# A fused attention and two-MoE kernel: a third value buffer, key and query loads three units ahead, and the pooled values' product moved one unit forward

## Chip, cores and metric

The kernel runs on one core of a Trainium2 chip. The metric is device time in microseconds (us) of one execution. Lower is better. TensorE is called PE, VectorE DVE, ScalarE ACT, GpSimd POOL; SP is the engine whose queue issues nearly all loads.

## What is computed

Three layers follow each other on 2304 tokens of width 512. The change touches the first alone: for 4 batches and 8 heads, an attention over mean-pooled tokens (groups of 4, 144 of them) is repeated to full length and added to a local attention in a band of 3 to each side. A soft MoE and a top-2 MoE (8 experts of 512x1024x512 each) come after it.

```python
q_d, k_d, v_d = (t.reshape(B, H, Sd, 4, D).mean(axis=3) for t in (q, k, v))
out_up = np.repeat(sm_attn(q_d, k_d, v_d), 4, axis=2)
scores = np.where(abs(pos[:, None] - pos[None, :]) < 4, scale * q @ k.T, -1e9)
x = out_up + softmax(scores) @ v
x = soft_moe(x, phi, w1, w2)          # 8 experts, 4 slots each
out = top2_moe(x, w_gate, w_noise, noise, w1, w2)
```

## The kernel before

**Units.** The attention is cut into 16 units, one for each batch and pair of heads. The work of a unit u is cut into named steps, and a table BL gives each step its function and an offset: at pass p of the loop over units (lines 592 to 615) a step with offset o works on unit p - o. The string SEQ (lines 19 and 20) is the order in which a pass writes its steps; every engine runs its own instructions in just that order, for a manual schedule is in force. The last pass is written out by TSEQ (lines 21 to 24), with a unit's number beside each step.

**The steps that matter here.** `ld` (load, line 186) issues four loads of a unit's keys and queries from SP, each of 96x6x64 floats in rows of 256 bytes (147,456 bytes); the tile `ld` has two buffers. `A0` and `A1` (a_pe) transpose keys and queries on PE (line 236) into PSUM tiles `t`, of which there are four; `a00`, `a01` and `a100` to `a111` copy them to K and Q. `S` (b_s) makes the local scores (lines 287, 292), `SD` (b_d) the pooled ones (line 303). `CP`, `CD` transpose the two probabilities; `EP00` to `EP11`, `ED0`, `ED1` copy them to PT and PdT. `lV` (load_v, line 202) issues four loads of a unit's values, each of 64x5x64 floats in rows of 256 bytes (81,920 bytes). `VD` (v_pe) pools the values, `V0`, `V1` copy the pooled values to Vd. `DP` (d_pe, line 416) is the local product of probabilities and values, `DD` (d_d, line 423) the pooled one; both go to the PSUM tiles xa and xb. `x0`, `x1` copy the local result to xT, `XA` (d_add, line 435) adds the pooled one to it. `EP`, `X0`, `X1`, `LG`, `LA` turn the result and multiply it with the router of the first MoE; once in four units `SE`, `ST`, `SS`, `SU_`, `SK` bring a batch into that MoE's slots.

**Who copies.** Function cp (line 222) sends a PSUM copy to ACT, unless its name is in the list ON_V (line 26): then DVE does it.

**Loads beside the attention.** `W` issues loads of the first MoE's weights (8 matrices of 2 MB in halves of 1,048,576 bytes, numbers 0 to 7) at a rate that NW (line 29) gives for each pass: one half a pass. Eight small loads (gate weights and noise, rows of 32 bytes) go out one a pass from pass 5 on. Values alternate between two buffers, so `lV` of unit u waits for `DP` of unit u - 2. Step R2 of TSEQ closes the attention's pools and loads weights 8 to 10 (w8a to w10b) into their place; weights 11 to 15 follow in the buffers of weights 0 to 4 as the first MoE's matmuls (lines 800 and 824) set them free. The second MoE's weights follow on the same queue.

The table's lines that place the moved steps:

```python
BL = {"ld": (load, -2, ()), "lV": (load_v, -1, ()), ...
      "DP": (d_pe, 1, ()), "DD": (d_d, 2, ()), "XA": (d_add, 2, ()), ...
for p in range(-1, NU - 1):
    if p >= 5 and small:
        o, i = small.pop(0)
        nc.sync.dma_start(out=o, in_=i)
    for nm in SEQ:
        f, off, a = BL.get(nm, (None, 99, ()))
        ...
            f(p - off, *a)
        if nm == "W" and p >= 0:
            flush(NW[p])
```

Of the kernel before, what the change touches and what calls it, by code (L numbers as in the profile page):

```python
# [7 lines left out]
F32 = mybir.dt.float32  # L8
# [10 lines left out]
SEQ = """DM ld S DD A0 M a00 a01 A1 a110 XA a100 SD EL a101 ST a111 SK CP SS EX W VD EP01 MD V0 EP00 EP10 SU_ LG CD EP11  # L19
EP V1 LA ED0 DX SU KD ED1 DP lV x1 x0 DQ1 X0 SE DQ0 RD P0 X1 P1""".split()  # L20
TSEQ = """S:15 DD:13 XA:13 DM:14 CP:14 W EP01:14 EP00:14 SD:15 M:15 EL:15 EP10:14 EX:15 EP11:14 CD:14 ED0:14 MD:15 SU:15 VD:14 DP:14 V0:14 V1:14 EP:13
# [4 lines left out]
ON_V = ['k1', 'd1', 'a101', 'a111', 'v0']  # L26
ON_V_END = ['P0', 'k1', 'v0', 'v1']

NW = [1] * 15
# [9 lines left out]
def attn_moe_moe_kernel(ctx: ExitStack, tc: tile.TileContext, q, k, v, moe_phi, moe_w1, moe_w2,  # L39
                        w_gate, w_noise, noise, w1, w2, out, dbg=None):  # L40
    nc = tc.nc
    B, H, S, D = q.shape
    NT = B * S
    DM = H * D
# [73 lines left out]
    with ExitStack() as tctx:  # L118
# [37 lines left out]
        Vs = [(a1, a2)[i].tile([128, 5, 2, D], F32, name=f"V{i}") for i in range(2)]  # L156
# [45 lines left out]
        def load_v(u):  # L202
            b, hp = units[u]
            V = Vs[u % 2]
            hv = v[b, 2 * hp:2 * hp + 2]
            for h in range(2):
                for g2 in range(2):

                    j0, j1 = int(u == h == g2 == 0), 5 - int(u == NU - 1 and h == g2 == 1)
                    rows = slice(64 * g2, 64 * g2 + 64)  # L210
                    t0 = 58 * (2 * j0 + g2) - 3
                    nc.sync.dma_start(out=V[rows, j0:j1, h], in_=bass.AP(
                        tensor=hv.tensor, offset=hv.offset + (h * S + t0) * D,
                        ap=[[D, 64], [116 * D, j1 - j0], [1, D]]))
                    if j0:
                        nc.sync.dma_start(out=V[3:64, 0, h], in_=hv[h, 0:61])
                    if j1 < 5:
                        nc.sync.dma_start(out=V[64:121, 4, h], in_=hv[h, S - 57:S])

# [46 lines left out]
        def v_pe(u):  # L266

            V = Vs[u % 2]
# [138 lines left out]
        def d_pe(u):  # L407
            b, hp = units[u]
            V = Vs[u % 2]
# [139 lines left out]
        def ok(u):  # L549
            return 0 <= u < NU  # L550

        load(0)

        BL = {"ld": (load, -2, ()), "lV": (load_v, -1, ()), "EP": (e_pe, 2, ()), "LG": (logit_pe, 2, ()),
# [8 lines left out]
              "DD": (d_d, 2, ()), "XA": (d_add, 2, ()), "VD": (v_pe, 1, ()), "V0": (v_evac, 1, (0,)), "V1": (v_evac, 1, (1,)),  # L563
# [28 lines left out]
        for p in range(-1, NU - 1):  # L592
            if p == 0:
                nc.sync.dma_start(out=phi, in_=moe_phi.rearrange("(k p) s -> p k s", p=128))
            if p >= 5 and small:
                o, i = small.pop(0)
                nc.sync.dma_start(out=o, in_=i)
# [812 lines left out]
```

## Time and profile before

| | |
|---|---|
| time, median of 3 runs | 489.71 us (487.59 to 493.68) |
| profiled execution: its time | 488.25 us |
| profiled execution: its span | 486.5 us |
| around the span (difference) | 1.75 us |
| PE, DVE, ACT, POOL busy in the span | 94%, 57%, 56%, 46% |
| attention: first local scores of unit 0, of unit 15 | 6.98 us, 137.51 us |
| first matmul of the first MoE | 159.94 us |
| end of the first MoE's second layer | 192.42 us |
| first matmul of the top-2 MoE's output layer (line 1061) | 208.90 us |

The span runs from the first to the last instruction. A busy time is a sum over an engine's instructions. PE's ends are modelled, so a matmul that stands still inside a run of matmuls can count as busy. In a timeline a row is a run of like instructions: its start, its length, engine, line, operation, tiles, sizes, how many; in square brackets the idle time of the engine ahead of it and what ended that.

### The profile page before, as it was taken

Reading aid. Unit: us, or ns where it says so; the run is one execution under the profiler, and the core shown is the slowest. Engines: PE = TensorE matmul, PEld = TensorE weight load, DVE = VectorE, ACT = ScalarE, POOL = GpSimd, SP = SyncE. Lnnn points to the kernel's source line nnn. Section 1 sums busy time; section 2 is a strip of 40 time slices with the busy share of each in tenths; the row PEclk is TensorE's granted clock in tenths of the full one; section 3 lists DMA queues with packets and bytes.
Section 4 is the critical chain, followed back from the end, with each engine's and each line's share of the span. In section 5 each row is a group of like instructions: output and inputs, shape, how many; then the busy total and the mean of one; then the engine's idle time right before and its main releaser. Section 6 shows DMA issues by size and latency. Waiting matters only on the chain.

```text
span 486.5 us, 12430 instructions
## 1 busy us (share of the span) xinstructions
PE 458.1 (94%) x4765; PEld 355.7 (73%) x4765; DVE 275.1 (57%) x703; ACT 270.5 (56%) x699; POOL 221.9 (46%) x321
## 2 busy tenths in 40 slices
PE   6999998899888999999999999999999999999992
PEld 5788877778765543577777887887887877878882
DVE  6888676887875321886487463382552634615300
ACT  2687777777765112674484453672755646727310
POOL 7897667577631201084766677222222222212232
PEclk9999899999999999999999999999999999999998
DMA  8999999899979999999986843799958855333333
GB/s 161 234 245 204 249 207 204 222 224 232 251 212 377 378 394 395 372 341 353 355 236 183 244 67 62 214 357 265 274 98 220 201 129 139 45 43 45 44 44 46
DMA packets 107977, 104.19 MB, mean 214 GB/s; under 512 B 67722, under 2 KB 77642, under 8 KB 107914
## 3 DMA queue, kind: packets, MB, share of 16 engines
q1 hardware_dynamic: 101002, 90.50, 62.5%
q0 software_dynamic: 6912, 12.85, 17.6%
q8 instruction: 40, 0.66, 0.6%
q14 instruction: 23, 0.19, 0.1%
HBM read 83.60 MB, written 19.73 MB: 212 GB/s over the span
## 4 chain that ended last, share of the span: by engine, by line
PE 42%; issue 8%; POOL 2%; POOLq 2%; DVE 1%; DMA 1%; ACT 1%; DVEq 0%
PE y L1061 34%; PE gx L878 2%; PE h L1041 2%; POOL out_dram L1080 2%; POOLq L1086 1%; PE gx L1041 1%; DMA out_dram<-ys,idx 1%; PE xs L944 1%; DVE hl L1043 1%; PE xs L1022 0%; PE xs L941 0%; ACT ys L1072 0%; DVE wlo L1033 0%; PE gx L958 0%; ACT hh L1042 0%
## 5 line engine op out<-in xcount | busy, mean ns | idle before, releaser
L1061 PE MATMUL y<-whi,hl 128*128 128x512 f32 x320 | 127.3, 398 | 0.0
L1061 PE MATMUL y<-whi,hh 128*128 128x512 f32 x320 | 126.6, 396 | 0.4 <-ACT hh L1042 0.4
L1061 PE MATMUL y<-wlo,hh 128*128 128x512 f32 x320 | 126.6, 396 | 0.0
L1080 POOL DMA_INDIRECT out_dram<-ys,idx x40 | 64.6, 1614 | 108.5 <-ACT ys L1072 62.6
L1072 ACT ACTIVATE ys<-y,gt 128x512 f32<-128x512 f32 x40 | 27.4, 686 | 83.7 <-issue 46.9
L1033 DVE TENSOR_TENSOR wlo<-wr,whi 128x512 fp32r<-128x512 f32 x64 | 42.0, 692 | 49.3 <-ACT whi L1030 41.7
L1061 PEld LDWEIGHTS y<-wlo,hh 128*128 128x128 f32 x320 | 60.1, 188 | 12.9 <-issue 1.0
L1061 PEld LDWEIGHTS y<-whi,hl 128*128 128x128 f32 x320 | 60.1, 188 | 12.3 <-issue 2.1
L1061 PEld LDWEIGHTS y<-whi,hh 128*128 128x128 f32 x320 | 60.2, 188 | 11.8 <-ACT hh L1042 0.6
L1007 POOL DMA_INDIRECT tab<-stk,pos x36 | 35.8, 994 | 11.5 <-issue 10.4
L1043 DVE SCALAR_TENSOR_TENSOR hl<-h,hh 128x256 fp32r<-128x256 f32 (+1 forms) x64 | 31.4, 490 | 16.0 <-ACT hh L1042 10.6
L1043 DVE SCALAR_TENSOR_TENSOR hl<-gx,hh 128x256 fp32r<-128x256 f32 (+1 forms) x64 | 31.2, 488 | 10.7 <-ACT hh L1042 7.4
L1030 ACT ACTIVATE whi<-wr 128x512 fp32r<-128x512 f32 x64 | 36.9, 625 | 0.2
L1042 ACT ACTIVATE hh<-gx 128x256 fp32r<-128x256 f32 (+1 forms) x64 | 28.1, 439 | 15.0 <-PE gx L1041 12.0
L1042 ACT ACTIVATE hh<-h 128x256 fp32r<-128x256 f32 (+1 forms) x64 | 28.0, 437 | 12.5 <-PE h L1041 9.5
L236 PE MATMUL t<-idf,ld 96*128 96x96 f32 x192 | 23.7, 270 | 11.8 <-DMA ld<-in_q_dram 5.6
L1079 POOL MEMSET spacer<- 1x1 f32 x40 | 13.5, 338 | 40.9 <-issue 40.9
L236 PEld LDWEIGHTS t<-idf,ld 96*128 96x128 f32 x192 | 18.8, 153 | 16.4 <-DVE fa L166 4.3
L254 POOL TENSOR_TENSOR s<-Q 64x288 f32<-64x288 f32 x31 | 29.3, 945 | 2.4
L336 POOL TENSOR_TENSOR P<-El,su 64x350 f32<-64x350 f32 x31 | 24.4, 787 | 11.4 <-DVE Vd L226 4.9
L224 ACT ACTIVATE PT<-t 64x384 f32<-64x384 f32 (+1 forms) x64 | 25.9, 429 | 6.2 <-PE t L378 5.0
L926 DVE TENSOR_TENSOR oh<-iot,R 128x256 fp32r<-128x256 f32 (+2 forms) x50 | 20.5, 446 | 12.7 <-PE xs L944 10.3
(312 smaller groups left out, 877.9 us busy)
## 6 DMA issues: line engine op xcount, KB each, us to landing
wr<-in_moe_w_dram SPq DMA_DIRECT2D x88, 256.0 KB
wr<-in_moe_w_dram SPq DMA_DIRECT2D x40, 512.0 KB
wr<-in_moe_w_dram SPq DMA_DIRECT2D x16, 1024.0 KB
out_dram<-zero SPq DMA_DIRECT2D x20, 256.0 KB
V<-in_v_dram SPq DMA_DIRECT2D x62, 80.0 KB
ld<-in_k_dram SPq DMA_DIRECT2D x32, 144.0 KB
ld<-in_q_dram SPq DMA_DIRECT2D x32, 144.0 KB
XT<-tab SPq DMA_DIRECT2D x5, 320.0 KB
```

What stands on the lines that cost most here:

```text
L224: nc.scalar.activation(dst, src, AF.Copy)
L236: nc.tensor.transpose(t[:, 96 * c:96 * c + 96], ld[:, i, 3 * j + c].rearrange("p h d -> p (h d)"), idf[0:96, 0:96])
L254: nc.gpsimd.tensor_tensor(q2, q4[:, :, 0:2], q4[:, :, 2:4], op=ALU.add)
L336: eng.tensor_tensor(P[as_, :, HQ * a:HQ * a + KW], El[as_], su[as_, :, None].to_broadcast([64, NG, KW]), op=ALU.mult)
L1007: st = nc.gpsimd.indirect_dma_start(out=tab, out_offset=bass.IndirectOffsetOnAxis(ap=pos[:, c, i:i + 1], axis=0), in_=stk[:, i].bitcast(F3 ...
L1030: nc.scalar.activation(whi[:, kk], wb(kk), AF.Copy)
L1033: eng.tensor_tensor(wlo[:, kk], wb(kk), whi[:, kk].bitcast(F32), op=ALU.subtract)
L1042: nc.scalar.activation(hh[:, f], h, AF.Relu)
L1043: nc.vector.scalar_tensor_tensor(hl[:, f], h, 0.0, hh[:, f].bitcast(F32), op0=ALU.max, op1=ALU.subtract)
L1061: nc.tensor.matmul(y, l[:, kk, ts_], r_[:, kk], start=(m == 0), stop=(m == 23))
L1072: nc.scalar.activation(ys, YS.pop((e, ti)), AF.Copy, scale=gt[:, ti:ti + 1])
L1080: st = nc.gpsimd.indirect_dma_start(out=out, out_offset=bass.IndirectOffsetOnAxis(ap=idx[:, ti:ti + 1], axis=0), in_=ys, in_offset=None, c ...
```

## The change

1. Values have three buffers in place of two, so `lV` of unit u waits for `DP` of unit u - 3.
2. `ld` loads unit p + 3 at pass p (before: p + 2), and stands in SEQ behind `A1`, which frees its buffer; units 0 and 1 are both loaded ahead of the loop. `lV` and `W` come right behind it. SP's queue has them in the order keys and queries, values, weights.
3. NW gives no weight half to pass 0, one to passes 1 to 12 and two to passes 13 and 14. The eight small loads go out four at a time, at passes 13 and 14.
4. `DD` and `XA` have offset 1: they work on the unit whose `DP` stands in the same pass, and leave TSEQ's head for unit 13.
5. SEQ is another order, and ON_V holds other copies: p10, p11 (two copies to PT) and k0 (128x512 to xK) go to DVE, a111 (a copy to Q), v0 (Vd 128x128), d1 (PdT 16x288) and k1 (64x128 to xK) to ACT.

```diff
-SEQ = """DM ld S DD A0 M a00 a01 A1 a110 XA a100 SD EL a101 ST a111 SK CP SS EX W VD EP01 MD V0 EP00 EP10 SU_ LG CD EP11
+SEQ = """S A0 A1 ld lV W M a101 SD DM a00 SS a01 EL a100 a110 ST SK a111 CP EP01 EP10 EP11 VD EP00 MD KD SU_ LG CD V1 V0
...
-ON_V = ['k1', 'd1', 'a101', 'a111', 'v0']
+ON_V = ['p10', 'p11', 'k0', 'a101']
...
-NW = [1] * 15
+NW = [0] + [1] * 12 + [2] * 2
...
-        Vs = [(a1, a2)[i].tile([128, 5, 2, D], F32, name=f"V{i}") for i in range(2)]
+        Vs = [(wk, a1, a2)[i].tile([128, 5, 2, D], F32, name=f"V{i}", bufs=1) for i in range(3)]
...
-            V = Vs[u % 2]
+            V = Vs[u % 3]
...
         load(0)
-
-        BL = {"ld": (load, -2, ()), "lV": (load_v, -1, ()), "EP": (e_pe, 2, ()), "LG": (logit_pe, 2, ()),
+        load(1)
+
+        BL = {"ld": (load, -3, ()), "lV": (load_v, -1, ()), "EP": (e_pe, 2, ()), "LG": (logit_pe, 2, ()),
...
-              "DD": (d_d, 2, ()), "XA": (d_add, 2, ()), "VD": (v_pe, 1, ()), "V0": (v_evac, 1, (0,)), "V1": (v_evac, 1, (1,)),
+              "DD": (d_d, 1, ()), "XA": (d_add, 1, ()), "VD": (v_pe, 1, ()), "V0": (v_evac, 1, (0,)), "V1": (v_evac, 1, (1,)),
...
-            if p >= 5 and small:
+            for _ in range(4 if p >= NU - 3 else 0):
```

**SP, one pass in the middle of the attention.** Before, the queue of SP reads as follows; `ld` are keys and queries, V0 and V1 the two value buffers, `wr` a weight half.

```order
L191 DMA ld_493<-in_k_dram 96x6x64 x2
L191 DMA ld_493<-in_q_dram 96x6x64 x2
L102 DMA wr_169<-in_moe_w1_dram 128x2x1024
L212 DMA V1_136<-in_v_dram 64x5x64 x4
L191 DMA ld_667<-in_k_dram 96x6x64 x2
L191 DMA ld_667<-in_q_dram 96x6x64 x2
L102 DMA wr_170<-in_moe_w1_dram 128x2x1024
L212 DMA V0_135<-in_v_dram 64x5x64 x4
```

And now, with V0, V1 and V2 in turn:

```order
L191 DMA ld_541<-in_k_dram 96x6x64 x2
L191 DMA ld_541<-in_q_dram 96x6x64 x2
L212 DMA V0_135<-in_v_dram 64x5x64 x4
L102 DMA wr_174<-in_moe_w1_dram 128x2x1024
L191 DMA ld_715<-in_k_dram 96x6x64 x2
L191 DMA ld_715<-in_q_dram 96x6x64 x2
L212 DMA V1_136<-in_v_dram 64x5x64 x4
L102 DMA wr_175<-in_moe_w1_dram 128x2x1024
```

The kinds and counts of a pass are the same; the values stand ahead of the weight half, the keys and queries are those of one unit later, and the values' buffer is one that was read a unit earlier.

**PE, from one unit to the next.** The difference on PE where the local product of one unit (line 416) meets the next unit's local scores (lines 287, 292):

```order
 L416 MATMUL xa<-PT,V_135 64x58 x2
 L416 MATMUL xb<-PT,V_135 64x58 x2
+L423 MATMUL xb<-PdT,Vd 64x144 x4
 L287 LDWEIGHTS idb
 L287 MATMUL S<-mask,idb 64x350
@@ -59,5 +60,4 @@
 L287 MATMUL S<-mask,idb 64x350
 L292 MATMUL S<-K,Q 64x35 x20
-L423 MATMUL xb<-PdT,Vd 64x144 x4
 L236 MATMUL t<-idf,ld 128x96 x12
```

The pooled product (four matmuls) moves from behind the next unit's scores to the place right behind the local product; nothing else on PE changes its place within a unit.

**ACT, one unit.** Before, ACT runs a unit without slot work in this order:

```order
L224 ACTIVATE K<-t 128x288 x2
L224 ACTIVATE Q<-t 64x288 x2
L322 ACTIVATE El<-El 128x350
L224 ACTIVATE PT<-t 64x3x128 x2
L224 ACTIVATE PT<-t 64x2x128 x2
L224 ACTIVATE Vd<-xb 16x128
L224 ACTIVATE PdT<-t 128x288
L354 ACTIVATE Ed,sumd<-Sd,nmd 96x144 x3
L224 ACTIVATE xT<-xb 128x5x58
L224 ACTIVATE xT<-xa 128x5x58
L224 ACTIVATE xK<-t 128x4x128
```

And now:

```order
L224 ACTIVATE K<-t 128x288 x2
L224 ACTIVATE Q<-t 64x288 x3
L224 ACTIVATE PT<-t 64x3x128 x2
L224 ACTIVATE Vd<-xb 16x128
L224 ACTIVATE Vd<-xa 128x128
L322 ACTIVATE El<-El 128x350
L224 ACTIVATE PdT<-t 128x288
L224 ACTIVATE PdT<-t 16x288
L354 ACTIVATE Ed,sumd<-Sd,nmd 96x144 x3
L224 ACTIVATE xT<-xa 128x5x58
L224 ACTIVATE xT<-xb 128x5x58
L224 ACTIVATE xK<-t 64x128
```

Both inputs of the pooled product (Vd and PdT) now come from ACT alone, each behind more work than before, and the exponential of the local scores (El) comes behind the copies to PT.

## Rows read from the trace of the kernel before

**Rows 1.** Stretches: length, busy PE, PEld, DVE, ACT, POOL, granted clock, DMA share, GB/s.
```profile
20.00:36.00 16.00, 15.49 (x325) 13.71 (x320) 13.07 (x35) 13.37 (x43) 14.63 (x23) 1.00 1.01 245
20.00:136.00 116.00, 106.44 (x2118) 91.16 (x2113) 91.18 (x231) 87.58 (x284) 83.35 (x121) 0.99 1.01 229
...
136.00:144.00 8.00, 6.64 (x154) 5.75 (x155) 5.49 (x15) 4.53 (x15) 2.45 (x3) 1.00 0.54 142
144.00:192.00 48.00, 46.59 (x745) 23.88 (x735) 16.94 (x61) 14.69 (x41) 7.94 (x32) 1.00 1.03 385
...
48.00:50.00 2.00, 1.22 (x10) 1.09 (x11) 1.04 (x2) 0.71 (x2) 0.60 (x1) 0.88 0.84 286
50.00:52.00 2.00, 2.00 (x12) 1.99 (x11) 0.91 (x2) 1.22 (x3) 0.07 (x1) 0.50 1.12 316
52.00:54.00 2.00, 2.00 (x40) 1.72 (x38) 1.81 (x3) 1.16 (x3) 1.61 (x3) 0.77 1.06 150
```

**Rows 2.** PE's timeline in the attention, some units.
```profile
22.46 0.34 PE L287 MATMUL S<-mask,idb 128*64 128x350 bf16 x2
...
23.77 0.69 PE L423 MATMUL xb<-PdT,Vd 128*64 128x144 f32 x8
...
29.85 0.34 PE L287 MATMUL S<-mask,idb 128*64 128x350 bf16 x2
...
56.41 0.34 PE L287 MATMUL S<-mask,idb 128*64 128x350 bf16 x2
...
65.36 0.34 PE L287 MATMUL S<-mask,idb 128*64 128x350 bf16 x2
...
118.94 0.34 PE L287 MATMUL S<-mask,idb 128*64 128x350 bf16 x2
...
122.51 0.69 PE L236 MATMUL t<-idf,ld 96*128 96x96 f32 x6 [0.93 <-DMA ld<-in_q_dram]
...
127.45 0.34 PE L287 MATMUL S<-mask,idb 128*64 128x350 bf16 x2
...
137.51 0.34 PE L287 MATMUL S<-mask,idb 128*64 128x350 bf16 x2
```

**Rows 3.** PE's waits from 14 to 140 us: total, times, longest.
```profile
PE t L236 <- DMA ld<-in_q_dram: 5.3, 7, 1.1
PE S L292 <- issue: 1.8, 2, 1.4
PE t L236 <- DMA ld<-in_k_dram: 1.0, 2, 0.6
```

**Rows 4.** SP's timeline at the attention's end.
```profile
130.61 0.60 SPq L102 DMA_DIRECT2D wr<-in_moe_w_dram  x1
137.59 2.61 SPq L212 DMA_DIRECT2D V<-in_v_dram  x4
...
141.20 3.41 SPq L104 DMA_DIRECT2D w8a<-in_moe_w_dram  x4
...
161.07 3.91 SPq L104 DMA_DIRECT2D wr<-in_moe_w_dram  x8
```

**Rows 5.** Copies that change engine, 20 to 137 us: busy, mean ns, idle before.
```profile
L224 ACT ACTIVATE Q<-t 64x288 f32<-64x288 f32 x26 | 11.2, 432 | 6.5 <-PE t L236 5.3 <-POOL s L262 0.8
...
L224 ACT ACTIVATE PT<-t 64x256 f32<-64x256 f32 x28 | 10.4, 372 | 0.3
...
L224 ACT ACTIVATE xK<-t 128x512 f32<-128x512 f32 x12 | 7.1, 595 | 0.0
...
L226 DVE COPY PdT<-t 16x288 f32<-16x288 f32 x13 | 5.0, 383 | 0.0
...
L226 DVE COPY Vd<-xa 128x128 f32<-128x128 f32 x14 | 3.9, 279 | 0.0
...
L226 DVE COPY xK<-t 64x128 f32<-64x128 f32 x12 | 3.0, 253 | 0.0
```

**Rows 6.** ACT's timeline: the copy to PdT ahead of the scores at 118.94 us.
```profile
117.72 0.38 ACT L224 ACTIVATE PdT<-t 128x288 f32<-128x288 f32 x1
```

More of the change, by code (lines that the diff above doesn't have):

```diff
@@ L17 @@
 CAP = 640
-SEQ = """DM ld S DD A0 M a00 a01 A1 a110 XA a100 SD EL a101 ST a111 SK CP SS EX W VD EP01 MD V0 EP00 EP10 SU_ LG CD EP11
-EP V1 LA ED0 DX SU KD ED1 DP lV x1 x0 DQ1 X0 SE DQ0 RD P0 X1 P1""".split()
-TSEQ = """S:15 DD:13 XA:13 DM:14 CP:14 W EP01:14 EP00:14 SD:15 M:15 EL:15 EP10:14 EX:15 EP11:14 CD:14 ED0:14 MD:15 SU:15 VD:14 DP:14 V0:14 V1:14 EP:13
+SEQ = """S A0 A1 ld lV W M a101 SD DM a00 SS a01 EL a100 a110 ST SK a111 CP EP01 EP10 EP11 VD EP00 MD KD SU_ LG CD V1 V0
+EP EX DP ED0 ED1 LA X0 DX DD x0 x1 X1 SE DQ0 DQ1 SU RD P0 XA P1""".split()
+TSEQ = """S:15 DM:14 CP:14 W EP01:14 EP00:14 SD:15 M:15 EL:15 EP10:14 EX:15 EP11:14 CD:14 ED0:14 MD:15 SU:15 VD:14 DP:14 V0:14 V1:14 EP:13
 ED1:14 P0:15 P1:15 DD:14 DX:15 LG:13 X0:13 RD:15 x0:14 DM:15 x1:14 CP:15 LA:13 EP00:15 X1:13 EP01:15 EP11:15
@@ L266, in v_pe @@
         def v_pe(u):
-            V = Vs[u % 2]
+            V = Vs[u % 3]
             XL[u] = [ps.tile([128, 512], F32, name=n) for n in ("xa", "xb")]
@@ L408, in d_pe @@
             b, hp = units[u]
-            V = Vs[u % 2]
+            V = Vs[u % 3]
             xl = XL[u]
```

## Prediction, made blind

> **What bounds the kernel now.** I read the stretches first, then PE's timeline in the attention, then PE's waits, then SP's timeline. The stretches [rows 1] show two regimes. From 20 to 136 us, the attention, the load engines are busy all the time (share 1.01) but move only 229 GB/s; from 144 to 192 us, while the first MoE's weights stream, the same share moves 385 GB/s. The attention's rows of 256 bytes are what is slow. PE is busy 106.44 of 116.00 us in the attention, so PE and loads both stand near their limit there, and neither alone explains the time.
>
> PE's timeline [rows 2] tells them apart. One unit runs from one row of line 287 to the next. With nothing late a unit takes 29.85 - 22.46 = 7.39 us. A unit with slot work takes 65.36 - 56.41 = 8.95 us, 1.56 more. A unit in which the queries arrive late takes 127.45 - 118.94 = 8.51 us, 1.12 more, of which 0.93 is shown as idle, waiting on `ld`. From unit 2 (22.46) to unit 15 (137.51) there are 115.05 us for 13 units, three of them with slot work; at the undisturbed pace they would take 13 x 7.39 + 3 x 1.56 = 100.75. So at most 14.3 us can be won between these two marks. PE's waits [rows 3] explain part: 5.3 + 1.0 = 6.3 us for queries and keys, in nine waits; 1.8 us are "issue", which no load named here ends.
>
> [...]
>
> **Why the loads are late.** Before, a unit's `ld` goes out one pass ahead of its use and behind the values of the unit before, and those values wait until the local product two units back has freed their buffer. At the end this shows most plainly: SP issues a weight half at 130.61 and the last values only at 137.59 [rows 4]; the stretch from 136 to 144 us moves 142 GB/s at a share of 0.54 [rows 1].
>
> **The change part by part**, against the profiled execution (488.25 us: 486.5 of span and 1.75 around it).
>
> *Loads one unit earlier, three value buffers.* No bytes are added. Keys now have about two passes to arrive in, some 15 us in place of 7, and values wait for a product that is long over. All nine waits on `ld` should go: -6.3. A late unit loses 1.12 for 0.93 of idle, a fifth more than is shown: another -1.3. The fall of the clock followed such waits (PE's idle stretch at 48 to 50 us): -1.7. Together -9.3; the bounds are 0 (the loads only queue longer) and the whole 14.3 of excess.
>
> *What is late next: the load engines themselves.* A unit's loads are 4 x 147,456 + 4 x 81,920 + 1,048,576 = 1,966,080 bytes. From 20 to 36 us, while PE kept its pace, they moved 245 GB/s at a share of 1.01 [rows 1]; at that rate a unit takes 8.02 us, 0.63 more than PE's 7.39. Over passes 1 to 12 that is a debt of 12 x 0.63 = 7.6 us. Pass 0 loads no weights now, which gives 1.05 MB at 385 GB/s = 2.7 back, and the two slot units among them give 2 x 1.56 = 3.1. What is left, 1.8 us, I charge: +1.8, with bounds 0 and +7.6.
>
> The row for 20 to 36 us leaves 8.02 - 2.72 = 5.3 us for 917,504 bytes in rows of 256 bytes, 173 GB/s [rows 1]. [...]
>
> *Two weight halves in passes 13 and 14, and the small loads there.* Those passes have no keys to load, so the 2.7 us of the second half takes the place of `ld`. Ahead of the values of unit 15 stand eight small loads and two extra halves; these values are first used by `VD` in the last pass, behind that unit's scores, more than a pass later. I take 0. If the cover goes, the price is one half, +2.7.
>
> *The pooled product and the add at their own unit's end.* The product takes 0.69 us and starts 23.77 - 22.46 = 1.31 us behind the scores [rows 2]; now it comes in front of them. PE does as much as before: the last pass loses one product (-0.69), pass 1 gains one (+0.69). What is added is a wait: PE stands at it until ACT has copied both PdT parts and both Vd parts, and the next unit's scores and key transposes are queued behind it on PE, then ACT's and POOL's work on those keys. Before, PdT's larger copy ended at 117.72 + 0.38 = 118.10 and the scores began at 118.94 [rows 2, 6], 0.84 us later. Ahead of the end of the second PdT copy, ACT now has one Q copy, one Vd copy and the small PdT copy more, and two small PT copies less: 0.432 + 0.279 + 0.383 - 2 x 0.372 = +0.35 [rows 5]. So PdT is whole about 0.5 us before PE comes to the product, which stands where the scores stood. I charge +0.3 in all. The bounds are -0.7, if pass 1's product hides in that pass's own waits, and 14 units x 0.38 = +5.3, if PE waits out one whole PdT copy each time.
>
> *Copies that change engine.* ACT loses 2 x 0.372 + 0.595 = 1.34 us a unit and gains 0.432 + 0.279 + 0.383 + 0.253 = 1.35 [rows 5], with DVE's durations taken for ACT; DVE the reverse. ACT is busy 13.37 of 16.00 us at PE's pace [rows 1], so 1.2 us of each 7.39 stay free: 0, covered by that.
>
> *Behind the attention.* Weights 8 to 10 fill the place of the attention's tiles and weights 11 to 15 wait until the first MoE's matmuls free their buffers: the first such load went out at 161.07, in a stream that had not paused since 144 us [rows 1, 4]. If all before it lands sooner than PE arrives, the stream pauses there and has to start again: +0.8, between 0 and +1.1, the time from the first MoE's first matmul (159.94) to that load's issue. Everything later moves with PE's arrival, for the load queue runs on behind it in the same order.
>
> *Sum:* -9.3 + 1.8 + 0.3 + 0.8 = -6.4, so 481.85 us for an execution like the profiled one. That one lies 1.46 us under the median of the runs, so the median comes to 489.71 - 6.4 = 483.3 us. A measurement of this kernel tells about 2% (9.8 us) from no change.
>
> **The rivals.**
>
> *The load engines are already full.* For it: a share of 1.01 over the whole attention [rows 1], and depth adds no rate. A unit then stays at 115.05 / 13 = 8.85 us. Only the hole from 136 to 144 us closes, worth 8 x (1 - 142 / 385) = 5.0 us of loading, but PE's last pass does not wait for those bytes, so little comes of it: I give it -0.7, 489.0 us. Against it: the 245 GB/s of 20 to 36 us at that same share.
>
> *The pace is PE's throughout.* If the debt is covered by the head start and the "issue" idles vanish with the crowding, unit 15's scores come at 22.46 + 100.75 = 123.2 in place of 137.51: -14.3, +0.8 for the restart, 476.2 us; 475 to 480 when a few waits stay. For it: three units in a row at that pace early on. Against it: the debt of 0.63 a unit.
>
> *The pooled product becomes the wait, and the kernel slower.* Place: line 423, now between local product and next scores, behind ACT's longer chain. If ACT, once the loads no longer hold PE back, runs late by as much as a late unit loses today (1.12 us, rows 2), 14 units cost 15.7 us; less the 6.4 won that is +9.3, 499.0 us. It decides from 6.4 / 14 = 0.46 us a unit on, and makes the kernel 2% slower from 1.16. For it: the margin of half a microsecond is worked out, not seen. Against it: ACT's free 1.2 us a unit.
>
> **How the numbers follow.** Forecast (480 to 487.5) 0.47; load engines full 0.20; PE's pace throughout 0.22; pooled product slower 0.11. Faster by over 2% means under 479.9: nearly all of the third case and a little of the first, 0.27. Slower by over 2% means over 499.5: the upper half of the last, 0.06. Within 2%: 0.67. The range goes from 475.5, inside the third case, to 491.0, which takes in the second and leaves out most of the last. The forecast's own range is 480 to 487.5.
>
> **What would show it.** [...] Wrong: waits on `ld` as long as before (engines full), waits of PE at line 423 on ACT's copies of PdT or Vd of half a microsecond and more, or an earlier end of the attention that is lost again between the first MoE and the top-2 MoE.

## The result, and the profile after

The changed kernel takes 495.28 us (491.89 to 498.52, 20 runs), the kernel before beside it 490.77 us (487.19 to 494.87, 20 runs). The ratio is 1.0109, with an interval of 1.0085 to 1.0133: slower by about 1%, which is less than 2% and yet clear of the noise. I had forecast 483.3 us and a range of 475.5 to 491.0; the change went the other way. The ratios, here and below, are those of fast executions and are not the quotient of the two medians.

The profiled execution of after took 496.65 us (span 494.2). It lies 1.4 us above the median of after, and the profiled one of before (488.25) 2.5 us under the median beside it: the two traces are 8.4 us apart where the medians are 4.5 apart. So marks from these two traces show where time is lost, and overstate how much.

The stretches of after, with the columns of [rows 1]:

```profile
2.00:20.00 18.00, 12.77 (x136) 10.39 (x137) 13.52 (x33) 6.07 (x19) 12.04 (x25) 1.00 0.86 165
20.00:36.00 16.00, 16.00 (x310) 14.20 (x308) 13.30 (x33) 12.51 (x42) 14.66 (x22) 1.00 0.89 194
20.00:136.00 116.00, 110.42 (x2191) 97.23 (x2189) 86.89 (x225) 86.63 (x304) 85.34 (x124) 0.97 0.92 210
136.00:144.00 8.00, 6.43 (x146) 5.62 (x138) 5.95 (x18) 4.96 (x20) 3.21 (x4) 1.00 0.93 286
144.00:156.00 12.00, 9.05 (x157) 6.24 (x158) 5.89 (x23) 6.84 (x22) 1.15 (x2) 1.00 0.75 269
156.00:192.00 36.00, 33.41 (x509) 14.60 (x503) 9.25 (x31) 5.92 (x12) 3.59 (x26) 1.00 1.04 394
...
110.00:112.00 2.00, 2.00 (x41) 1.93 (x38) 0.75 (x1) 0.49 (x2) 0.59 (x1) 0.51 0.73 225
```

Two stretches of before that stand in no group:

```profile
2.00:20.00 18.00, 15.09 (x167) 12.35 (x167) 14.15 (x40) 6.41 (x20) 14.26 (x28) 1.00 1.04 209
144.00:156.00 12.00, 10.59 (x198) 7.45 (x192) 7.47 (x29) 8.77 (x29) 2.39 (x3) 1.00 1.02 376
```

PE is busier in the attention than before (110.42 against 106.44 us, though some of it at a lower clock: 0.97), as the forecast wanted. The load engines are not: their share fell from 1.01 to 0.92 and the rate from 229 to 210 GB/s [rows 1]. By 136 us they have moved (209 - 165) x 18 + (229 - 210) x 116 = 3.0 MB less; by 156 us, with the rows for 136 to 156 us, it is 3.1 MB.

PE's waits from 14 to 150 us:

```profile
PE xb L423 <- issue: 2.2, 1, 2.2
PE xa L273 <- DMA V<-in_v_dram: 1.9, 1, 1.9
PE t L378 <- POOL P L336: 1.6, 1, 1.6
PE t L378 <- POOL kd L263: 1.2, 1, 1.2
PE t L236 <- DMA ld<-in_q_dram: 0.9, 1, 0.9
PE S L292 <- issue: 0.8, 1, 0.8
```

Of the 6.3 us on keys and queries [rows 3], 0.9 are left. But the first MoE shows what came of it. PE's timeline there:

```profile
159.92 2.37 PE L801 MATMUL hp<-wr,sinT 128*32 128x256 f32 x40
...
187.64 0.64 PE L801 MATMUL hp<-wr,sinT 128*32 128x256 f32 x8 [0.64 <-DMA wr<-in_moe_w_dram]
...
191.00 1.05 PE L825 MATMUL yacc<-wr,hz 128*32 128x512 f32 x2 [0.29 <-DMA wr<-in_moe_w_dram]
...
193.36 6.14 PE L825 MATMUL yacc<-wr,hz 128*32 128x512 f32 x21
199.43 0.77 PE L759 MATMUL ct<-idf,LK 128*128 128x128 f32 x5
```

PE begins the first MoE at 159.92 us, within 0.02 us of before. It ends it at 199.43 in place of 192.42, 7.0 us later, waiting for weights. Its last run of 21 matmuls lasts 6.14 us, but that is no sign of the change: it stands in before too.

```profile
186.19 6.30 PE L824 MATMUL yacc<-wr,hz 128*32 128x512 f32 x21
```

At this end PE waits for weights 11 to 15 in both kernels. What moved is the moment from which they are loaded. SP's timeline of after says why:

```profile
127.86 0.47 SPq L598 DMA_DIRECT2D wgn<-in_moe_w_gate_dram  x1
...
130.27 4.95 SPq L212 DMA_DIRECT2D V<-in_v_dram  x4
135.28 1.16 SPq L102 DMA_DIRECT2D wr<-in_moe_w_dram  x2
136.48 5.23 SPq L598 DMA_DIRECT2D nz<-in_moe_noise_dram  x4
141.81 4.66 SPq L212 DMA_DIRECT2D V<-in_v_dram  x4
146.57 0.43 SPq L218 DMA_DIRECT2D V<-in_v_dram  x1
147.04 0.89 SPq L102 DMA_DIRECT2D wr<-in_moe_w_dram  x2
148.03 2.09 SPq L104 DMA_DIRECT2D w8a<-in_moe_w_dram  x4
...
167.23 36.64 SPq L104 DMA_DIRECT2D wr<-in_moe_w_dram  x44
```

In before, w8a went out at 141.20 [rows 4]; now two halves stand at 147.04, w8a at 148.03. The row at 167.23 is the first load of weights 11 to 15, which went out at 161.07 before [rows 4]. It needs the buffer of weight 0, which PE's first matmuls set free, and its turn in SP's queue. Before, it went out 1.13 us behind PE's first matmul (159.94); now it goes out 7.31 us behind it, for w8a to w10b are issued first and were late. The queue is 6.8 us late at w8a, 6.2 us at 167.23, and the first MoE ends 7.0 us late.

### The profile page after: what moved, and what is told of

Read it like the earlier page. It is cut to its first block, busy times and chain, and to the rows that moved or that the text cites. A ratio compares the mean times of both kernels' runs of the same rounds, so it can differ in the third digit from the quotient of the medians.

```text
span 494.2 us, 12408 instructions
## 1 busy us (share of the span) xinstructions
PE 463.2 (94%) x4765; PEld 359.6 (73%) x4765; DVE 270.0 (55%) x688; ACT 267.8 (54%) x714; POOL 219.5 (44%) x321
## 4 chain that ended last, share of the span: by engine, by line
PE 41%; issue 8%; POOL 2%; POOLq 2%; DVE 1%; ACT 1%; DMA 1%; DVEq 0%
PE y L1062 34%; PE gx L879 2%; PE h L1042 2%; POOL out_dram L1081 2%; POOLq L1087 1%; PE gx L1042 1%; DMA out_dram<-ys,idx 1%; PE xs L945 1%; DVE hl L1044 1%; PE xs L1023 0%; PE xs L942 0%; ACT ys L1073 0%; DVE wlo L1034 0%; ACT hh L1043 0%; PE gx L959 0%
## 5 line engine op out<-in xcount | busy, mean ns | idle before, releaser
L1044 DVE SCALAR_TENSOR_TENSOR hl<-h,hh 128x256 fp32r<-128x256 f32 (+1 forms) x64 | 31.3, 490 | 16.5 <-ACT hh L1043 13.6
L1044 DVE SCALAR_TENSOR_TENSOR hl<-gx,hh 128x256 fp32r<-128x256 f32 (+1 forms) x64 | 31.2, 488 | 10.7 <-ACT hh L1043 7.4
L236 PE MATMUL t<-idf,ld 96*128 96x96 f32 x192 | 22.7, 273 | 5.7 <-DMA ld<-in_k_dram 4.4
L927 DVE TENSOR_TENSOR oh<-iot,R 128x256 fp32r<-128x256 f32 (+2 forms) x50 | 20.9, 450 | 11.1 <-PE xs L945 8.4
L292 PE MATMUL S<-K,Q 128*64 128x35 f32 x640 | 23.2, 232 | 3.2 <-DVE Q L226 2.4
L292 PEld LDWEIGHTS S<-K,Q 128*64 128x64 f32 x640 | 23.4, 147 | 3.7 <-issue 3.6
```

Of the source, the lines that this page charges most:

```text
L236: nc.tensor.transpose(t[:, 96 * c:96 * c + 96], ld[:, i, 3 * j + c].rearrange("p h d -> p (h d)"), idf[0:96, 0:96])
L292: nc.tensor.matmul(s[64 * a:64 * a + 64, KW * g:KW * g + KW], Q[:, c0:c0 + 32].rearrange("p i h -> p (i h)"), K[:, c0:c0 + KW], start=Fals ...
L1044: nc.vector.scalar_tensor_tensor(hl[:, f], h, 0.0, hh[:, f].bitcast(F32), op0=ALU.max, op1=ALU.subtract)
```

## The experiments

All ratios are to the kernel before, run beside on the same chip; an interval follows in brackets. The median of before ranged from 489.58 to 493.54 us in these sets of runs, so ratios can be compared and times cannot. "Loads" means part 1 to 3 of the change, "compute" part 4 and 5 (with the order of the steps).

**Loads or compute.** e3_compute_alone has after's compute with before's loads, e4_loads_alone the reverse.

```diff
 # e4: before, with
-SEQ = """DM ld S DD A0 M a00 a01 A1 a110 ...
+SEQ = """DM S DD A0 M a00 a01 A1 ld lV W a110 ...
 # and three buffers, load(1), NW and the small loads of after
```

> Loads exactly as in the kernel before (two value buffers, keys two units ahead, the old order on SP and the old schedule), with the changed kernel's compute order, copies and pooled product at its own unit's end. Theories A and B: the loss is in the loads, so this stays at the time of before, 490 to 492. Theory C: it is as slow as the changed kernel, 494 to 496.

> Loads exactly as in the changed kernel, with the compute order, copies and pooled product of the kernel before. Theories A and B: as slow as the changed kernel or slower, 494 to 497, with the first MoE's weights 2 to 3 MB behind at 156 us. Theory C: the time of before, 490 to 491, or faster since no wait on keys is left.

Measured: compute 493.74 us, 1.0038 [1.0003, 1.0072]; loads 494.8 us, 1.0079 [1.0038, 1.0119]. By the middle values the loads carry most of it, though the two intervals overlap. In e4 PE began the first MoE at 160.05 us and ended it at 199.59, as in after: the late stream belongs to the loads alone. With compute alone weights 11 to 15 follow PE's first matmul as in before (1.13 us), and still 0.4% is lost.

**Which part of the loads.** Both are after with one part undone.

```diff
 # e1_w_before_v
-SEQ = """S A0 A1 ld lV W M
+SEQ = """S A0 A1 ld W lV M
 # e2_schedule_old
-NW = [0] + [1] * 12 + [2] * 2
+NW = [1] * 15
-            for _ in range(4 if p >= NU - 3 else 0):
+            for _ in range(1 if p >= 5 and small else 0):
```

> The changed kernel with each pass's weight half issued between keys and values instead of behind the values. The trace of the changed kernel shows the first MoE's weights 2.7 MB behind at 156 us, 7.0 us at 385 GB/s, and its end 7.0 us late, though PE reaches it at the same time (159.92 against 159.94 us). Theory A, order within a pass: four value loads are issued alone, one per 0.6 us and more, and nothing large moves beneath them; with a weight half ahead of them the engines stay full: 4 to 6 us faster than the changed kernel, so 489 to 491 us, and the share of 20 to 136 us comes back to 1.0 from 0.92. Theory B, schedule over passes (none in pass 0, small loads and two halves at the end): no more than 1.5 us faster, 494 to 495. Theory C, compute order (product, copies, start): no change, 495.

> The changed kernel with the old schedule over passes: one weight half in each pass from pass 0, small loads one a pass from pass 5. Theory A: 0 to 1.5 us faster than the changed kernel, 494 to 495. Theory B: the half of pass 0 (1.05 MB, 2.7 us at 385 GB/s) and the last passes' idle loading (0.33 share and 0.31 to 0.35 share in 134 to 136 and 144 to 148 us, some 3 us) come back: 4 to 6 us faster, 489 to 491. Theory C: no change, 495.

Measured: 494.71 us, 1.0047 [1.0002, 1.0092], and 493.88 us, 1.0043 [1.0006, 1.008]. Against after's 1.0109, from another set of runs, each gives back some 0.6%; for e1 the intervals still touch. The weights' mark moves as it should: w8a goes out at 145.11 (order undone), 141.98 (schedule undone) and 138.81 us (both, in f1 below) in place of 148.03; 2.9 and 6.1 us, together 9.2. The time does not add up like that: f1, with both undone, stands at 1.0045 and gives back no more than either. Neither theory alone was right. Order and schedule together make the stream late enough to matter; with one of them undone it is in time, and what stays is about what compute alone costs. In e1 the old order cost something else: the values of unit 15 came behind small loads and two halves, and PE waited 4.96 us for them at 150.37, in the last pass:

```profile
150.37 1.08 PE L273 MATMUL xa<-V,four 128*32 128x128 f32 x16 [4.96 <-DMA V<-in_v_dram]
```

**Is the depth worth something once the stream is mended?** f1_depth_only is after with e1 and e2 together. f2_depth_late_memset puts POOL's early memsets late again too. f3_depth_old_compute is before with three buffers and keys a unit deeper. f4_three_buffers is before with the third buffer alone.

```diff
 # f2, over f1
-                if p == -1 and nm == "lV":
+                if p == -1 and nm == "LA":
 # f3, over before
-SEQ = """DM ld S DD A0 M a00 a01 A1 a110 ...
+SEQ = """DM S DD A0 M a00 a01 A1 ld W lV a110 ...
+        load(1)
-        BL = {"ld": (load, -2, ()), ...
+        BL = {"ld": (load, -3, ()), ...
-                if p == -1 and nm == "lV":
+                if p == -1 and nm == "KD":
 # f3 and f4, over before
-        Vs = [(a1, a2)[i]. ... for i in range(2)]
+        Vs = [(wk, a1, a2)[i]. ... bufs=1) for i in range(3)]
```

> The changed kernel with the weight half of a pass put back between the keys and the values, and with the old schedule (a half in each of the 15 passes, small loads one a pass from pass 5). What stays of the change: three value buffers, keys one unit deeper, and all of its compute order. Stream theory (the loss comes from weights that are asked for later than before): the stream catches up with before's, w8a goes out at 141 to 144 us, the first MoE ends at 193 to 196 us, the ratio to before is 0.997 to 1.003. Compute theory (the new order on PE, ACT and DVE costs 0.4% by itself, whatever the loads): the ratio stays at 1.004 to 1.006, PE reaches the first MoE at 162 us or later, though few waits on ld are left.

> The kernel f1_depth_only with the three early memsets on POOL hung on a late step of the pass ahead of the loop, where before has them. Start theory: line 166 on DVE takes about 0.9 us again in place of 2.5, the scores of unit 1 come at about 14.5 to 15 us in place of 16.5, and the time is 1.0 to 1.5 us under that of f1 (0.2 to 0.3%). Rival: the time that is won at the start is lost at the first wait on a load, and f2 is equal to f1 within 0.5 us from unit 3 on.

> The kernel before, order of its compute and its copies untouched, with three value buffers, keys one unit deeper (ld behind A1, then the weight half, then the values) and its own schedule of weights and small loads. The first step of my prediction alone: the nine waits on ld (6.3 us) go, PE reaches the first MoE 3 to 9 us sooner. If the first MoE's end follows PE's arrival, the time is 3 to 7 us under before (ratio 0.986 to 0.994). Rival, the load engines are the bound: PE comes sooner, but w8a goes out at 141 us or later as before, the first MoE ends at 191 to 193 us, and the ratio is 0.998 to 1.002.

> The kernel before with a third value buffer and nothing else. If the buffers held the values back: SP's stop of several us ahead of the last values goes, w8a goes out 2 to 5 us sooner than at 141 us, the waits on ld get no shorter, and since PE's arrival sets the first MoE's end in before, the time gets at most 1 us shorter (ratio 0.998 to 1.001). If the load engines were full all along: w8a stays at 140 to 142 us.

Measured: f1 495.48 us, 1.0045 [1.0013, 1.0078]; f2 495.31 us, 1.0019 [0.998, 1.0058]; f3 494.99 us, 1.003 [0.9994, 1.0067]; f4 492.67 us, 0.9987 [0.9953, 1.002]. The lines with `KD` and `lV` keep POOL's memsets in f3 as late as before has them. Had the waits on `ld` been all that held PE, f3 would have been 3 to 7 us faster; it is not faster at all. In f2 line 166 took 0.93 us again and unit 1's scores came at 15.81 in place of 16.68, but the times of f1 and f2 can't be told apart. In f4 w8a went out at 134.20, 7 us sooner than in before, and the first MoE ended 0.9 us sooner: as long as PE comes last there, earlier weights are worth next to nothing, for weights 11 to 15 wait for PE's first matmuls all the same.

f3's waits of PE, 14 to 140 us, show what took the place of the loads:

```profile
PE S L292 <- issue: 4.0, 3, 1.6
PE t L236 <- issue: 2.8, 2, 1.5
PE xb L416 <- issue: 2.1, 1, 2.1
PE xa L416 <- issue: 1.5, 1, 1.5
PE xa L416 <- DVE Vd L226: 0.3, 1, 0.3
```

No wait on `ld` is left, and 10.4 us are "issue", where before had 6.3 on `ld` and 2.7 of "issue": the 1.8 of [rows 3] and

```profile
PE xb L416 <- issue: 0.9, 1, 0.9
```

These idles have a pattern. Stretches of f3 from 0 to the end of an idle (PE's and PEld's counts in brackets are what matters here):

```profile
0.00:49.77 49.77, 41.08 (x714) 35.18 (x714) 37.02 (x101) 30.24 (x93) 39.97 (x71) 1.00 0.97 206
0.00:77.13 77.13, 67.11 (x1210) 57.48 (x1211) 57.09 (x156) 50.60 (x159) 58.71 (x98) 0.98 1.01 212
0.00:85.18 85.18, 73.62 (x1333) 63.19 (x1334) 63.67 (x172) 55.79 (x176) 63.95 (x106) 0.98 1.01 213
...
0.00:113.06 113.06, 98.34 (x1830) 84.24 (x1830) 85.39 (x228) 76.29 (x243) 83.61 (x134) 0.98 0.99 215
```

PE has run 1428, 2421, 2667 and 3660 matmuls and weight loads when these idles end: 993, 246 and 993 apart. Counted with PE's sequencer instructions, which this view leaves out, they lie 1024, 256 and 1024 instructions apart, and all eight idles of f3 lie a multiple of 256 apart (each within one). The instruction queue brings 0.66 MB in 40 packets. A packet starts in the half microsecond from 82.3 us, takes 1.3 us, and the idle behind it ends at 85.19:

```profile
85.19 0.21 PE L416 MATMUL xa<-PT,V 64*64 64x58 f32 x1 [1.54 <-issue]
```

Over f3, every idle on issue ended 1.3 to 1.8 us behind the end of such a packet. From the place where PE entered one block of 256 to the start of the packet that brought the next, about 3 us went by on the mean and up to 6. So the reading is: PE runs out of instructions, because their packet stands behind data. It holds for the other kernels too: before's three idles on issue, after's three of 0.4 us and more, and such idles of every other run with rows of 256 bytes stand at that same place in a block of 256 (within one), 1.2 to 1.8 us behind the end of a packet.

**Taking data away.** g1_no_weights is f3 with no weight half during the attention; g3_no_values is f3 with values loaded for units 0 to 2 alone, the later ones using those again.

```diff
 # g1
-NW = [1] * 15
+NW = [0] * 15
 # g3
             hv = v[b, 2 * hp:2 * hp + 2]
+            if u >= 3:
+                return
```

> The kernel f3_depth_old_compute without any weight half during the attention; all of them are asked for behind it, so its total time is no answer, only PE's pace up to the scores of unit 15 is. In f3 every idle of PE put down to issue (10.8 us, eight of them) ended 1.3 to 1.8 us behind the end of one packet of the instruction queue, and stood at PE instructions that lie 256 or a multiple of 256 apart. Theory: PE runs out of instructions because the packet with the next 256 waits behind data (3.1 us on the mean from the place where PE entered the 256 before it to the packet's start). Then with half the bytes gone that wait falls under 1.5 us, the idles on issue under 2 us, and the scores of unit 15 come at 123 to 128 us in place of 140. Rival: PE runs its short matmuls faster than instructions can be fetched, whatever else moves: the idles on issue stay at 8 to 11 us, and unit 15 comes at 134 us or later.

> The kernel f3_depth_old_compute with the values loaded for units 0 to 2 alone (later units use those again, so the output is another); weights, keys and queries as in f3. It takes 4.9 of 31 MB out of the attention, all of it in rows of 256 bytes. If any load ahead of the instruction packet counts by the time that it takes: rows of 256 bytes take 5.3 of the 8 us of a unit's loads, the values 1.9 of them, so the wait of the packet falls from 3.1 to about 2 to 2.5 us and the idles on issue from 10.8 to 4 to 7 us. If only the weight halves hold it up: both stay as in f3.

Measured: in g1 both kinds of wait are gone up to unit 15's scores, at 124.82 us (140.34 in f3); the packets' wait fell from about 3 to about 1 us. The stretch and all of PE's waits, 14 to 126 us:

```profile
20.00:136.00 116.00, 114.92 (x2402) 99.03 (x2400) 99.32 (x259) 97.56 (x317) 89.02 (x128) 1.00 0.67 154
```

```profile
PE xa L416 <- DVE Vd L226: 0.3, 1, 0.3
PE xb L416 <- ACT Vd L224: 0.2, 1, 0.2
```

So neither fetching as such nor the compute limits PE to what before shows: with room on the load engines the same order runs at the undisturbed pace, 101.6 us from unit 2 to unit 15 against the 100.75 of my prediction. In g3 the packets' wait is about 2 us, the idles on issue 3.0 us, unit 15 at 129.02; the first MoE starts at 149.90 and ends at 182.36 us, both 13.2 us sooner than in f3, and the whole takes 478.94 us (one run; f3 has a median of 494.99). There w8a goes out at 122.09, so the weights keep up, and what PE gains in the attention does reach the end in full.

**Product, copies, start.** g4_product_alone moves `DD` and `XA` of before to their own unit's end; h4_copies_alone gives before the ON_V of after; g2_compute_late_memset is e3 with the late memsets.

```diff
 # g4, over before
-... ED1 DP lV x1 x0 DQ1 X0 SE DQ0 RD P0 X1 P1
+... ED1 DP DD lV x1 x0 DQ1 X0 SE DQ0 RD P0 X1 XA P1
-              "DD": (d_d, 2, ()), "XA": (d_add, 2, ()), ...
+              "DD": (d_d, 1, ()), "XA": (d_add, 1, ()), ...
 # h4, over before
-ON_V = ['k1', 'd1', 'a101', 'a111', 'v0']
+ON_V = ['p10', 'p11', 'k0', 'a101']
```

> The kernel before with the pooled product right behind its unit's local product and the addition in the same pass, and nothing else (copies, loads and their order as before). My prediction charged +0.3 us for it, with bounds -0.7 and +5.3. If PE waits there for ACT's copies of PdT and Vd: 0.2 to 0.4 us a unit, 3 to 5 us in all, ratio 1.005 to 1.01, and waits of PE at line 423 on ACT or DVE. If not: ratio 0.998 to 1.002 and no such waits above 0.5 us in all.

> The kernel before with the changed kernel's division of copies between ACT and DVE and nothing else (order and loads as before). The compute order as a whole costs 0.4 to 0.5% (e3_compute_alone, g2_compute_late_memset), the product alone nothing (g4_product_alone, 0.998), so what is left is the copies' engines or the order that they are written in. If the engines: ratio 1.003 to 1.006. If the order written: ratio 0.998 to 1.001, as I predicted for the copies (nothing).

> The changed kernel's compute order with the loads of before (the kernel e3_compute_alone, ratio 1.0038), and the three memsets on POOL at a late place again. Start theory: all that the compute order costs is the start (1.5 to 2 us up to the scores of unit 1), so the ratio is 0.999 to 1.001. Rival: the product at its own unit's end or the copies that change engine cost something in every unit, and the ratio stays at 1.003 or more.

Measured: product 491.98 us, 0.9978 [0.9933, 1.0023], no wait at line 423 on a copy; copies 491.89 us, 1.0007 [0.9965, 1.0048]; compute with late memsets 494.48 us, 1.0053 [1.0013, 1.0093]. The product and the copies cost nothing that the runs can tell. The edit of g2 changed next to nothing, for in e3 the memsets are late already: they begin at 7.54 us there and at 7.30 in g2, and line 166 takes 0.93 us in both. So g2 repeats e3. Both lose 0.4 to 0.5% with late memsets, so early ones are not what the compute order costs; the start theory fell by that. Which step of the new order costs the 0.4 to 0.5% stays open.

**Longer rows.** The last question was whether time on rows of 256 bytes is the common cause. h1_wide_before, h2_wide_depth and h3_wide_after load keys and queries six tokens to a row (1,536 bytes) in before, f3 and after; r2_row_pairs two tokens (512 bytes) in before. Each transpose then holds two tokens of one head, and copies of 64x288 spread them with a stride. ON_V gets one of the new copies to K in h1 to h3; in r2 it is d1, a110, a111, a010 and a011.

```diff
-  src[b, 2 * hp + h].rearrange("(c p) d -> p c d", c=6)
+  src[b, 2 * hp + h].rearrange("(p c) d -> p c d", c=6)             # h1 to h3
+  src[b, 2 * hp + h].rearrange("(c p e) d -> p c (e d)", c=3, e=2)  # r2
```

> The kernel before, its order and depth of loads untouched, with keys and queries loaded six tokens to a partition: rows of 1,536 bytes in place of 256. The transposes on PE stay as many; the copies to K become four of 64x288 in place of two of 128x288, one more on ACT and one more on DVE a unit (0.4 us each). If the time that the load engines spend on small rows is what bounds the attention (directly by waits on ld, and through the instruction packets behind them): a unit's loads fall from 8.0 to 6.0 to 6.5 us, under PE's 7.39; waits on ld under 1 us, idles on issue under 3 us, unit 15's scores at 124 to 130 us, the first MoE's end 5 to 10 us sooner, ratio 0.978 to 0.99. Rival: ACT or DVE, with 0.4 us more a unit, become the bound, or the strided writes are slow: a unit takes 7.8 us or more without any late load, ratio 0.995 or more.

> The kernel f3_depth_old_compute (three value buffers, keys one unit deeper) with the same rows of 1,536 bytes. If depth is worth something once the load engines have room: under h1_wide_before by 1 to 3 us. If the engines' time was all: equal to it within 0.3%. If depth costs by the instruction packets that wait behind more data: idles on issue greater than in h1_wide_before, and not faster than it.

> The changed kernel with the same rows of 1,536 bytes. If its loss comes from the load engines (weights asked for late, while small rows move slowly), the loss shrinks: within 0.4% of h1_wide_before, the cost of its compute order alone, and well under before. If the loss comes from the order of compute or from SP's stops at the gate whatever the load takes: again 1% over h1_wide_before.

> The kernel before with keys and queries in rows of 512 bytes (two tokens to a row), written back by copies of stride 2 and 4 elements in place of 6 and 12, where a copy took 0.68 us in place of 0.43; K's and Q's copies of one head on ACT, of the other on DVE, so that no copy waits for the other engine's. DVE has 0.3 us more a unit. If a row of 512 bytes takes about the time of one of 256, and the copies 0.43 us again: waits on ld and idles on issue under 2 us together, share of the load engines 0.8 to 0.9 from 20 to 136 us, unit 15's scores at 125 to 131 us, ratio 0.980 to 0.993. Rival: the copies stay near 0.68 us, the share falls but ACT and DVE set the pace, ratio 1.01 or more.

Measured: h1 1.0548 [1.0502, 1.0593], h2 1.046 [1.0409, 1.0512], h3 1.0285 [1.0239, 1.033], r2 1.0225 [1.0178, 1.0272]. All slower than before, by the rival: the copies. Two of these miss what I expected among themselves. h3 was to lie within 0.4% of h1 or 1% above it, and lies 2.6% under it: PE waits 11.1 us for copies of Q by DVE at lines 381 and 392 in h1 (14 to 140 us), and has no such wait above 0.2 us in h3, whose copies are divided as in after. And h2 lies 0.9% under h1, with intervals that just touch: as far as they tell, depth is worth something where the load engines have room (share 0.63 in h1, 0.75 in h2). ACT's rows in r2, 20 to 136 us:

```profile
L224 ACT ACTIVATE Q<-t 64x288 f32<-64x288 f32 x26 | 18.2, 700 | 0.6
L224 ACT ACTIVATE K<-t 64x288 f32<-64x288 f32 x24 | 10.3, 431 | 9.9 <-PE t L236 9.6
```

Q's copy went from 432 [rows 5] to 700 ns, and a unit takes 9.1 us. On the loads the expectation held: in r2 the engines' share from 20 to 136 us is 0.72 at 204 GB/s (before 1.01 at 229 [rows 1]), and there is no wait on `ld` or issue from 14 to 140 us. These runs don't show what longer rows would be worth with copies as quick as before.

**Together.** r1_buffers_product is before with f4 and g4.

> The kernel before with the two parts of the change that cost nothing by themselves: the third value buffer (f4_three_buffers, 0.9987) and the pooled product at its own unit's end (g4_product_alone, 0.9978). If they add: 0.994 to 0.999, faster by 0.5 to 3 us. If both are noise around nothing, or more loads in flight bring back idles on issue: 0.998 to 1.003.

Measured: 488.71 us, 0.9983 [0.9952, 1.0014]; waits on `ld` 8.0 and on issue 3.1 us. No version that computes the same was clearly faster than before; f4, g4, h4 and r1 equal it, some 1% under after.

**The marks in one table.** Times in us. Waits are PE's from 14 to 140 us; the first MoE runs from its first matmul to the start of line 758 (`ct`; in after 759), the first thing behind it; "weight 11 out" is the first load of weights 11 to 15. Each row is one execution, and executions of one kernel lie several us apart (before: 487.19 to 494.87); those of f1 and f4 are the quickest of twelve. So a difference of a few microseconds between two rows is not yet one between two kernels.

| | share, GB/s, 20 to 136 | `ld` + issue | w8a out | first MoE from, to | weight 11 out | from there to the end |
|---|---|---|---|---|---|---|
| before | 1.01, 229 | 6.3 + 2.7 | 141.20 | 159.94, 192.42 | 161.07 | 31.4 |
| after | 0.92, 210 | 0.9 + 3.4 | 148.03 | 159.92, 199.43 | 167.23 | 32.2 |
| e3 compute alone | 0.94, 218 | 8.0 + 0.0 | 143.93 | 163.92, 197.07 | 165.05 | 32.0 |
| g2 compute, late memsets | 0.98, 222 | 10.9 + 0.0 | 145.38 | 163.19, 195.81 | 164.32 | 31.5 |
| e4 loads alone | 0.93, 209 | 2.3 + 3.0 | 147.73 | 160.05, 199.59 | 167.58 | 32.0 |
| e1 weights before values | 0.98, 225 | 0.0 + 6.0 | 145.11 | 164.48, 196.97 | 165.61 | 31.4 |
| e2 old schedule | 0.95, 219 | 5.1 + 1.8 | 141.98 | 163.17, 195.53 | 164.30 | 31.2 |
| f1 depth only | 1.04, 230 | 0.0 + 8.4 | 138.81 | 161.45, 193.73 | 162.59 | 31.1 |
| f2 depth, late memsets | 0.99, 221 | 0.0 + 8.1 | 141.88 | 167.08, 199.66 | 168.21 | 31.5 |
| f3 depth, old compute | 1.03, 227 | 0.0 + 10.4 | 138.97 | 163.07, 195.52 | 164.20 | 31.3 |
| f4 three buffers | 1.07, 233 | 4.4 + 3.2 | 134.20 | 158.96, 191.53 | 160.10 | 31.4 |
| g4 product alone | 0.97, 221 | 9.3 + 0.8 | 143.19 | 162.56, 195.20 | 163.69 | 31.5 |
| h4 copies alone | 1.00, 223 | 7.8 + 0.0 | 143.31 | 161.26, 193.55 | 162.39 | 31.2 |
| r1 buffers and product | 1.02, 227 | 8.0 + 3.1 | 136.57 | 159.93, 192.35 | 161.06 | 31.3 |
| g3 no values | 0.85, 229 | 0.0 + 3.0 | 122.09 | 149.90, 182.36 | 151.04 | 31.3 |

Two readings. The first MoE ends 31.1 to 32.2 us behind the first load of weights 11 to 15, in every row. That load goes out 1.1 us behind PE's first matmul wherever w8a is out by 145.4 us, so there PE's arrival sets the end; in after and e4, with w8a at 148 us, SP's queue comes to it 7.3 and 7.5 us behind PE's arrival and sets the end. And where the weights of the first MoE are moved in time, PE waits 6 to 11 us in the attention, now for keys, now for its own instructions. It waits less only where less is moved: 4.3 and 5.3 us in after and e4, which leave weights for later, and 3.0 in g3.

## Why the prediction was wrong

*Loads one unit earlier (-9.3).* The first step held by its letter: the waits on `ld` went from 6.3 to 0.9 us in after and to nothing in f1 and f3. What failed is that I took an ended wait for a shorter attention. In after, units 2 to 15 took 111.92 us in place of 115.05 (scores at 24.70 and 136.62), and the start gave 2.2 of the 3.1 back; the last 0.9 went behind unit 15's scores, where PE waited 1.9 us for that unit's values. In f3, 6.3 us on `ld` became 7.7 us more on issue. I had set the 1.8 us of "issue" in [rows 3] aside as nothing that a load ends; they stand at the same place in a block of 256 as f3's, so they were the same shortage, and my rival "PE's pace throughout" even let them vanish with the crowding. With rows of 256 bytes the depth alone is worth nothing that the runs can see (f3 1.003, f4 0.9987), and it added no rate: 227 GB/s in f3 and 230 in f1, 229 before [rows 1].

*The clock (-1.7).* No run shows that a fall of the clock costs 1.7 us: the term was my estimate from the clock granted between 48 and 54 us [rows 1]. What the runs showed in its place is no gain: from 20 to 136 us it was granted at 0.97 in place of 0.99. Behind the idle on issue that ends at 109.43, it was granted at 0.51 in after's row for 110 to 112 us. In before the fall (0.50 from 50 to 52 us [rows 1]) stood behind a wait on `ld`; here it stands behind an idle that no load of keys ended.

*The load engines' debt (+1.8, bounds 0 and +7.6).* The debt was real, but I looked for it at PE. It is paid in weights: 3.0 MB at the 394 GB/s of 156 to 192 us are 7.6 us, and the first MoE ended 7.0 us late. Nor were the engines full, as the bound supposed. In one pass of after SP issues as follows, the values first and the weight half behind them:

```profile
55.37 6.29 SPq L212 DMA_DIRECT2D V<-in_v_dram  x4
61.71 0.61 SPq L102 DMA_DIRECT2D wr<-in_moe_w_dram  x1
```

Meanwhile, share and rate (the last two columns) were these:

```profile
58.00:60.00 2.00, 2.00 (x23) 2.00 (x22) 1.32 (x3) 1.51 (x5) 1.92 (x3) 1.00 0.62 84
60.00:62.00 2.00, 2.00 (x31) 1.00 (x28) 1.92 (x6) 1.95 (x8) 1.76 (x4) 1.00 0.43 87
62.00:64.00 2.00, 2.00 (x36) 1.53 (x35) 1.32 (x4) 1.03 (x5) 1.56 (x3) 1.00 0.51 107
```

Why the issuing of the values goes with so low a share is not shown. e1 puts the half ahead of the values again, gains 0.6% and has a share of 0.98 over the attention.

*Two halves in passes 13 and 14, and the small loads (0).* The loss on the loads came by this term, together with the order in a pass above, which had no term. I named the price ("one half, +2.7") for values that might come late, and not for the weights behind. The values did come late, by 1.9 us in after (line 273); the weights by 6.8. The schedule undone (e2) brings w8a out 6.1 us sooner and gives back 0.6%.

*Behind the attention (+0.8).* "Everything later moves with PE's arrival, for the load queue runs on behind it" is the step that failed and made the kernel slower. It holds in every row of the table but two, best of all in g3 (13.2 us sooner than f3 at both ends), but not in after and e4, where SP's queue reaches w8a some 7 us later. I let the term grow to +1.1 at most, the time from the first MoE's first matmul to the first load of weights 11 to 15. That time is 7.31 us in after: 6.2 more than before, where I had charged 0.8. I had written that the queue keeps its order, and not worked out when it gets there.

*The pooled product (+0.3) and the copies (0).* Right by the runs alone: 0.9978 and 1.0007, with no wait at line 423 on a copy (in e2 there is one of 1.3 us, on a copy to xT). The rival that made this the slow case did not occur; the slow case that did was none of my rivals.

*What had no term.* The order of the steps as such (part 5). Compute alone costs 0.4 to 0.5%, some 2 of the 4.5 us between the medians, and by which step stays open.

*What I did not see.* Three memsets on POOL hang on the step `lV` of the pass ahead of the loop, and part 2 puts `lV` early. They begin at 3.88 us in place of 7.27 (in e4 too, at 3.89), beside line 166 on DVE. Of after:

```profile
3.17 2.46 DVE L166 TENSOR_SCALAR fa<-fi 128x288 f32<-128x288 f32 x1
```

```profile
3.88 1.16 POOL L612 MEMSET PT<- 128x1280 f32 x1
4.98 0.19 POOL L613 MEMSET Vd<- 128x128 f32 x1
5.13 0.33 POOL L614 MEMSET PdT<- 128x288 f32 x1
```

It took 0.93 us before and ends now at 5.63, right behind the last memset (5.46); before's 0.93 us ended at 4.10, behind a memset that ended at 3.94. Why line 166 takes longer beside the memsets is not shown. PE's unit 2 came 2.2 us later for the whole start (24.70 against 22.46 [rows 2]), but f2 shows that undoing the memsets alone brings no time that can be told.

## What to carry to other kernels

Here the load engines (share 1.01) and PE (busy 106.44 of 116.00 us) both stood near their limit [rows 1], and a wait that was taken away at one place came back at another: in f3, 6.3 us on `ld` became 7.7 us more on issue. Before you count a wait as won, add up the bytes that must be through by each later mark, and see who is last there. Weights that were only needed later were the cover for small loads: with the half ahead of the values the share was 0.98 over the attention (e1), with the values ahead of it 0.92 (after). Asking for them behind the small loads, or in the last units, moved the bill to the next stage, 7.0 us at the first MoE's end. The bill was due where a load hung both on PE and on its turn in the queue, 7.31 us behind PE's first matmul in place of 1.13: there the later of the two counted. And read "issue" on PE as a possible wait for loads: look whether such idles stand a multiple of 256 instructions apart and whether an instruction packet ends just ahead of them, as here 1.2 to 1.8 us ahead. Not every such idle is one: h3's eight of 0.8 us, at line 381, stand at the same place of a unit, at no multiple of 256, and follow no packet.

## What the runs showed of the hardware

- PE's instructions came in packets on the load engines, 40 of 16,384 bytes in before and in after, by the places of the idles one for 256 instructions. They waited longer in the runs with more data on its way: about 1 us on the mean with the engines' share at 0.67 (g1), about 2 at 0.85 (g3) and about 3 at 1.01 and 1.03 (before, f3); PE's idles on issue from 14 to 140 us came to nothing in g1, 3.0 us in g3, 2.7 in before and 10.4 in f3. In f3, PE went on 1.3 us or more behind the packet's end each time.
- Copies from PSUM to SBUF of 288 fp32 a partition on ACT took 408 ns written in one piece (K in before), 432 ns at a write stride of 8 bytes and 700, 686 and 682 ns at 16, 24 and 48 bytes (r2, h1). A stride of two fp32 was nearly free here (24 ns), one of four was not (292 ns). Why is not shown.
- Issuing four loads of values took SP 6.29 us where four such loads took 2.61 at the end of before [rows 4], and the load engines' share fell to 0.43 meanwhile (60 to 62 us, above): here an issuer that was busy all the time was no sign of full engines.
